# Fused attention and two mixtures of experts on one core: token norms from a Gram matrix, and a new order for the first tiles of the last layer

## Chip, cores and metric

The kernel runs on one core of one Trainium2 chip. The metric is the device time in microseconds (us) of one execution; lower is better. An execution's time is a little longer than the span from its first to its last instruction, which is what a trace shows.

## What is computed

Windowed attention (4 batches, 8 heads, 576 positions, 64 wide, window 64) gives x of 2304 tokens by 512. A first mixture of experts (8 experts with 4 slots each, 32 slots in all) turns x into slot outputs `so` and mixes them for each token. A second mixture sends each token to its best expert:

```python
# first mixture, its end
c = softmax(x @ phi, over the 32 slots)          # tokens x 32
y = c @ slot_out                                 # tokens x 512; slot_out is "so" below, 32 x 512
# second mixture
xn = y / (norm(y, per token) + 1e-6)
logits = xn @ en.T / tau                         # 8 experts
expert_idx = argmax(logits); gate_w = softmax(logits)[expert_idx]
for e in range(8):
    mask = expert_idx == e
    if not mask.any(): continue
    h = relu(y[mask] @ w1[e])                    # 512 -> 1024
    out[mask] = gate_w[mask, None] * (h @ w2[e]) # 1024 -> 512
```

All arithmetic is kept at about float32 accuracy: where a matmul runs on `fp32r` operands, one or both of them are split into a high and a low part.

## The kernel before

Work is ordered by hand (`tc.manual_schedule`): every engine runs its instructions in the order in which the code emits them. Attention comes first, with the first mixture's routing worked in; then its two layers, `layer1` (L709) and `layer2` (L729), in which the weights of all eight experts are streamed; then the second mixture. Only the stretch from `layer2` on is touched by the change.

**The combine matrix.** `c` (tokens by 32) lies in 18 tiles of 128 tokens. For each three tiles `prepT` (L792, VectorE) writes c divided by its sum, four times side by side, `trT` (L796) transposes it on TensorE, and `combT` (L802) writes it to `cTs` through `split_rows` (L701): a ScalarE copy of the high part, then one VectorE instruction which by row puts the high part or the remainder. `layer2(16)` to `layer2(31)` are 16 steps of four column-tiled matmuls each; the `combT` and `prepT` of tiles 6 to 11 stand between its steps 18 to 20 (L836 to L841), those of tiles 12 to 17 behind it. After `layer2`, `so` is copied out of PSUM (L845 to L847), and a short chain over TensorE and VectorE finds the expert `e0` of the first token. SyncE reads that number from SBUF (L895) and issues the loads of that expert's weights in five chunks `CH` (L877) of 1, 1, 2, 2 and 2 blocks of 128 hidden columns: `w1e` and `w2e` by turns (L897).

**The second mixture.** Since y = c @ so, the kernel doesn't form y for the layer. It takes u = so @ w1 instead (32 rows), and h = relu(c @ u). In `ffn` (L998) a chunk goes through these steps:
- `u_part` (L1002): four matmuls with 32 columns each, one for each quarter of the 512 inputs, that land in four groups of 32 rows; a copy to SBUF; `u_sum` (L1015) adds the groups with one more matmul by `R4` and splits the rows into `ust`. With chunk 0, `u_part` also forms so @ en (8 logit columns, L1010).
- `up` (L1022): for 256 tokens, one matmul of 256 columns for each hidden block, ReLU to the high part on ScalarE (or VectorE), and the low part on VectorE (L1032).
- `split_w2` (L1035): w2 into a high part (VectorE) and a low part (GpSimd).
- `down` (L1043): for one tile of 128 tokens and one chunk, three matmuls of 512 columns for each hidden block (high by high, low by high, high by low). `fin` (L1058) multiplies by the gate `gm` and stores.

**Norms and logits.** For each of the 18 tiles `ynorm` (L959) forms y with a matmul of 512 columns, and squares and sums it on ScalarE from PSUM, or from a copy in SBUF. `logits2` (L922) is a matmul of 8 columns a tile. `choose` (K), `others` (O), `gates` (G) and `gates_now` (M) are short chains on VectorE (with one small matmul and an Exp) that count which experts are used and make `gm`.

**The order.** The string `SEQ` (L9) names the steps for tiles 0 to 3 (and `up` for tiles 4 and 5): U, S, W and P, Q, R are `u_part`, `u_sum`, `split_w2` and `up` of token blocks 0, 1, 2, each taking its next chunk; 0 to 3 are `down` of that tile and chunk; a, b, d, y, z are norms and g logits. After the string tiles 4 to 17 follow, 24 matmuls each, in a fixed order that nothing in the change touches. PSUM has two buffers under each of the names `tr`, `s`, `et` and `pv`; tile 4 needs the `pv` buffer that `fin` of an earlier even tile frees.

Of the kernel before, what the change touches and what calls it, by code (L numbers as in the profile page):

```python
# [19 lines left out]
def tile_kernel(ctx, tc, q, k, v, phi, w1, w2, emb, tau, w1b, w2b, out):  # L20
# [21 lines left out]
    def ps(tag):  # L42
        return pp.tile([128, 512], FP32, tag=tag, name=tag)
# [55 lines left out]
    with tc.manual_schedule():  # L99
# [583 lines left out]
        sel = cpool.tile([128, 32], FP32, name="sel")  # L683
        selT = cpool.tile([32, 128], FP32, name="selT")

        sel5 = cpool.tile([128, 5, 32], F32R, name="sel5")
        selh = [sel5[:, i:i + 4] for i in range(2)]
# [10 lines left out]
        for r in range(5):  # L698
            g.tensor_scalar(out=sel5[:, r], in0=sel, scalar1=float(r % 2 == 0), scalar2=None, op0=ALU.mult)
# [68 lines left out]
        c4b = [md[:, 1124 + 384 * n:1508 + 384 * n].rearrange("p (t r s) -> p t r s", t=3, r=4) for n in range(2)]  # L768
# [23 lines left out]
        def prepT(t0):  # L792
            nc.vector.tensor_tensor(out=c4b[t0 // 3 % 2], in0=c[:, t0:t0 + 3, :].unsqueeze(2).to_broadcast([128, 3, 4, 32]),
                                    in1=cr[:, 1, t0:t0 + 3].unsqueeze(2).unsqueeze(3).to_broadcast([128, 3, 4, 32]), op=ALU.mult)

        def trT(t0):  # L796
            p = ps("et")
            for t in range(3):
                nc.tensor.transpose(p[:, 128 * t:128 * t + 128], c4b[t0 // 3 % 2][:, t].rearrange("p r s -> p (r s)"), ident)
            return p  # L800
# [26 lines left out]
        prepT(6)  # L827
        so_ps = ps("pv")
        layer2(16)
        combT(3, pT2)  # L830
        prepT(9)
# [27 lines left out]
        soT = m2.tile([128, 4, 2, 4, 4], FP32, name="soT")  # L859
        sos = wa.tile([128, 4, DM], F32R, tag=f"s{NA + 1}", name="sos")  # L860
        sost = sos[:, 0]
        soh = [sos[:, 1 + i] for i in range(2)]
# [21 lines left out]
        pT2 = trT(15) if "h" not in SEQ else None  # L884

        def rest9():
            combT(9)
            prepT(15)

# [30 lines left out]
        lg2 = []  # L920

        def logits2(t0, t1):  # L922
            if t0 == 0:
                lg2.append(ps("et"))
            l2p = lg2[0]
            for t in range(t0, t1):
                nc.tensor.matmul(l2p[:, E * t:E * t + E], lhsT=cTs[:, 128 * t:128 * t + 128], rhs=ust[0][:, 128:128 + E], start=True, stop=True)
            if t1 == NT:
                l2 = l2p[:, 0:E * NT].rearrange("p (t e) -> p t e", t=NT)
                nc.vector.tensor_reduce(out=mx, in_=l2, axis=AX.X, op=ALU.max)  # L930
                nc.vector.tensor_tensor(out=ld_, in0=l2, in1=mx.unsqueeze(2).to_broadcast([128, NT, E]), op=ALU.subtract)
# [27 lines left out]
        def ynorm(t, held=False, tag="tr"):  # L959
            p = ps("s" if held else tag)  # L960
            nc.tensor.matmul(p, lhsT=cTs[:, 128 * t:128 * t + 128], rhs=sost, start=True, stop=True)
            if held:
                nc.vector.tensor_copy(out=acc[:, t, :], in_=p)

                def square(dve):
                    if dve:
                        nc.vector.tensor_tensor_reduce(out=acc[:, t, :], in0=acc[:, t, :], in1=acc[:, t, :], scale=1.0, scalar=0.0,
                                                       op0=ALU.mult, op1=ALU.add, accum_out=nrm[:, t:t + 1])
                    else:
                        nc.scalar.activation(out=acc[:, t, :], in_=acc[:, t, :], func=ACTF.Square, accum_out=nrm[:, t:t + 1])  # L970

                return square
            nc.scalar.activation(out=p, in_=p, func=ACTF.Square, accum_out=nrm[:, t:t + 1])

# [12 lines left out]
        w2l = [wa.tile([128, 4, 512], F32R, tag=f"s{n}", name="w2l") for n in (4, 5)]  # L987
# [3 lines left out]
        ust = [m2.tile([128, 128 * n + (0 if f0 else E)], F32R, name=f"ust{f0}") for f0, n in CH]  # L991
# [6 lines left out]
        def ffn(first):  # L998
# [3 lines left out]
            def u_part(q_, dve=False):  # L1002
                f0, n = CH[q_]
                h, o = divmod(f0, 4)
                p = ps("tr")
                for cc in range(4):
                    l = soT[:, cc].rearrange("p r j i -> p (r j i)")
                    nc.tensor.matmul(p[32 * cc:32 * cc + 32, 0:128 * n], lhsT=l, rhs=w1e[h][:, cc, 128 * o:128 * (o + n)], start=True, stop=True)
                    if first and q_ == 0:
                        nc.tensor.matmul(p[32 * cc:32 * cc + 32, 128:128 + E], lhsT=l, rhs=enT[:, cc, :], start=True, stop=True)  # L1010
                w_ = 128 * n + (E if first and q_ == 0 else 0)
# [3 lines left out]
            def u_sum(q_, dve=False):  # L1015
                f0, n = CH[q_]
                p = ps("tr")
                w_ = 128 * n + (E if first and q_ == 0 else 0)
# [55 lines left out]
            yt = list(range(NT)) if first else []  # L1074
            yl = []

            lgs = [(t, t + 3) for t in range(0, NT, 3)]
            at = dict.fromkeys("USWPQRT/", 0)

            def ys(held, tag):  # L1080
                r_ = ynorm(yt.pop(0), held, tag)
                if r_:
                    yl.append(r_)

            def group(t):
                q_ = at["/"]
                down(t, range(CH[q_][0], sum(CH[q_])))
                if q_ == NQ - 1:
                    fin(t)

            def gates_now():
# [3 lines left out]
                "a": lambda: ys(False, "pv"), "b": lambda: ys(False, "tr"), "d": lambda: ys(True, "s"), "y": lambda: yl.pop(0)(False), "z": lambda: yl.pop(0)(True),  # L1095
                "g": lambda: logits2(*lgs.pop(0)), "h": rest9, "c": lambda: combT(12, pT), "C": lambda: combT(15, pT2),
                "K": choose, "O": others, "G": gates}
# [72 lines left out]
```

## Time and profile before

| | us |
|---|---|
| median of 3 runs | 299.7 |
| lowest and highest of them | 297.91, 301.16 |
| the profiled execution | 296.67 |
| its span | 295.0 |

Times in the rows count from the start of the span. A row of a timeline or a chain gives its start, its length, the engine, the line and what it did, with "x3" for three instructions merged; in brackets stands how long the engine had been idle and who released it. PE is TensorE's matmuls, PEld its weight loads (which overlap), DVE VectorE, ACT ScalarE, POOL GpSimd, SPq SyncE's queue. PEclk is the granted TensorE clock as a share of full speed. A float32 matmul shows as two instructions.

### The profile page before, as it was taken

Reading aid. Unit: us, or ns where it says so; the run is one execution under the profiler, and the core shown is the slowest. Engines: PE = TensorE matmul, PEld = TensorE weight load, DVE = VectorE, ACT = ScalarE, POOL = GpSimd, SP = SyncE. Lnnn points to the kernel's source line nnn. Section 1 sums busy time; section 2 is a strip of 40 time slices with the busy share of each in tenths; the row PEclk is TensorE's granted clock in tenths of the full one; section 3 lists DMA queues with packets and bytes.
Section 4 is the critical chain, followed back from the end, with each engine's and each line's share of the span. In section 5 each row is a group of like instructions: output and inputs, shape, how many; then the busy total and the mean of one; then the engine's idle time right before and its main releaser. Section 6 shows DMA issues by size and latency. Waiting matters only on the chain.

```text
span 295.0 us, 7567 instructions
## 1 busy us (share of the span) xinstructions
PE 274.2 (93%) x2860; PEld 209.1 (71%) x2860; DVE 173.7 (59%) x678; ACT 129.1 (44%) x351; POOL 61.8 (21%) x139
## 2 busy tenths in 40 slices
PE   7699899989998998999999799989999999999991
PEld 6477688878877886663432477768888888888891
DVE  4779787877897787554660488598333333333210
ACT  3775876687658776261210585440122112121100
POOL 4546524433405420040200033330000000000000
PEclk9999999999999999999999999999999999999998
DMA  5999899989999999999993394001231101010111
GB/s 134 280 231 296 255 274 306 306 247 278 278 341 308 280 299 378 366 376 390 387 386 131 95 337 143 0 0 50 95 67 41 38 36 71 36 38 36 72 48 32
DMA packets 53659, 57.26 MB, mean 194 GB/s; under 512 B 21490, under 2 KB 34034, under 8 KB 53618
## 3 DMA queue, kind: packets, MB, share of 16 engines
q1 hardware_dynamic: 53472, 56.70, 60.8%
q8 instruction: 25, 0.41, 0.6%
q14 instruction: 16, 0.13, 0.1%
q10 hardware_dynamic: 146, 0.02, 0.0%
HBM read 51.99 MB, written 4.72 MB: 192 GB/s over the span
## 4 chain that ended last, share of the span: by engine, by line
PE 70%; DVE 11%; ACT 9%; DMA 4%; SPq 2%; issue 2%; POOL 1%; POOLq 0%; ACTq 0%
PE et L1054 16%; PE pv L1054 15%; PE pv L732 5%; PE pv L325 5%; ACT sm L279 4%; PE tr L217 3%; PE s L1026 3%; PE tr L713 2%; PE s L713 2%; PE et L292 2%; ACT ets L298 2%; PE s L262 2%; PE pv L382 2%; DVE sm L278 2%; DMA v<-in_v_dram 2%
## 5 line engine op out<-in xcount | busy, mean ns | idle before, releaser
L279 ACT ACTIVATE sm<-sm,nm 128x128 f32<-128x128 f32 x144 | 47.3, 391 | 23.7 <-DVE nm L278 23.4
L1032 DVE SCALAR_TENSOR_TENSOR h<-s,h 128x512 fp32r<-128x512 f32 (+1 forms) x39 | 25.2, 650 | 43.4 <-ACT h L1031 43.1
L1031 ACT ACTIVATE h<-s 128x512 fp32r<-128x512 f32 (+1 forms) x33 | 18.8, 572 | 65.2 <-PE s L1026 65.0
L278 DVE CUSTOM_DVE_ANT_0 sm<-s,mask 128x128 f32<-128x128 f32 x144 | 34.1, 286 | 10.8 <-PE s L268 6.4
L1054 PE MATMUL pv<-w2h,h 128*128 128x512 f32 x144 | 37.4, 396 | 0.0
L1054 PE MATMUL et<-w2h,h 128*128 128x512 f32 (+1 forms) x160 | 37.1, 370 | 0.0
L1054 PEld LDWEIGHTS et<-w2h,h 128*128 128x128 f32 x160 | 27.4, 188 | 5.2 <-ACT h L1031 0.4
L325 PE MATMUL pv<-v,ets 128*64 128x65 f32 x640 | 25.7, 226 | 4.7 <-ACT ets L298 3.3
L1054 PEld LDWEIGHTS pv<-w2h,h 128*128 128x128 f32 x144 | 26.4, 188 | 5.0
L325 PEld LDWEIGHTS pv<-v,ets 128*64 128x64 f32 x640 | 21.4, 137 | 11.2 <-ACT ets L298 8.2
L217 PE MATMUL tr<-ident,spare 128*128 128x128 f32 x120 | 19.3, 285 | 2.1 <-POOL spare L212 2.1
L186 POOL COPY v<-v 64x512 f32<-64x512 f32 x16 | 9.7, 607 | 52.8 <-DMA v<-in_v_dram 52.8
L298 ACT COPY ets<-et 128x512 f32<-128x512 f32 x32 | 18.3, 572 | 3.5 <-PE et L292 3.1
L212 POOL COPY spare<-spare 128x512 f32<-128x512 f32 x30 | 18.3, 610 | 6.4 <-PE tr L217 4.1
L1054 PE MATMUL et<-w2l,h 128*128 128x512 f32 (+1 forms) x80 | 19.4, 368 | 0.0
L292 PE MATMUL et<-ident,sm 128*128 128x128 f32 x128 | 19.3, 273 | 0.0
L1054 PE MATMUL pv<-w2l,h 128*128 128x512 f32 x72 | 19.1, 390 | 0.0
L1039 POOL TENSOR_TENSOR w2l<-w2e,w2h 128x1024 fp32r<-128x1024 f32 (+1 forms) x5 | 9.8, 1952 | 37.5 <-PE tr L1019 20.7
L312 DVE COPY xT<-tr 128x320 f32<-128x320 f32 (+1 forms) x31 | 14.0, 451 | 4.3 <-ACT ets L300 3.6
L337 DVE TENSOR_TENSOR x<-pv,rc 128x256 f32<-128x256 f32 (+1 forms) x32 | 15.7, 491 | 1.1
L1026 PEld LDWEIGHTS s<-cTs,ust 128*128 128x128 f32 x72 | 13.0, 189 | 4.1 <-DVE h L1032 1.5
L1026 PE MATMUL s<-cTs,ust 128*128 128x256 f32 x72 | 14.7, 287 | 1.1 <-DVE h L1032 1.1
(313 smaller groups left out, 457.8 us busy)
## 6 DMA issues: line engine op xcount, KB each, us to landing
w<-in_moe_w_dram SPq DMA_DIRECT2D x32, 1024.0 KB, 8.5
v<-in_v_dram SPq DMA_DIRECT2D x32, 128.0 KB, 4.7
spare<-in_q_dram SPq DMA_DIRECT2D x15, 256.0 KB, 7.1
spare<-in_k_dram SPq DMA_DIRECT2D x15, 256.0 KB, 5.7
out_dram<-acc SPq DMA_DIRECT2D x15, 256.0 KB, 2.1
w1e<-in_moe_w_dram SPq DMA_DIRECT2D x3, 512.0 KB
w2e<-in_moe_w_dram SPq DMA_DIRECT2D x3, 512.0 KB, 7.6
out_dram<-acc SPq DMA_DIRECT2D x6, 128.0 KB, 2.1
```

Source lines behind the costliest of these rows:

```text
L212: g.tensor_copy(out=perm[nm], in_=t)
L217: nc.tensor.transpose(po[:, r], perm[nm][:, r].rearrange("p h d -> p (h d)"), ident)
L278: nc.vector.tensor_tensor_reduce(out=sm[:, u], in0=s[h][:, a], in1=m, scale=-scale, scalar=3.0e38, op0=ALU.add, op1=ALU.min, accum_out=nm[ ...
L279: nc.scalar.activation(out=sm[:, u], in_=sm[:, u], func=ACTF.Exp, bias=nm[:, u:u + 1], scale=-1.0)
L292: nc.tensor.transpose(p[:, 128 * u:128 * u + 128], e[:, u, :], ident)
L298: nc.scalar.copy(out=o[:, 0:4], in_=p.rearrange("p (n h q) -> p n h q", n=4, h=2))
L325: nc.tensor.matmul(p[64 * par:64 * par + 64, a, h, :], lhsT=et[:, u, x, :], rhs=vt[:, sl, h, :], start=True, stop=True)
L337: nc.vector.tensor_tensor(out=x_tok[b, hp][:, js[0]:js[0] + nj].rearrange("p j (h d) -> p j h d", h=2), in0=p[:, :, :, 0:64], in1=rc[:, 0: ...
L1026: nc.tensor.matmul(p[:, 256 * i:256 * i + 256], lhsT=ucol[f0 + i], rhs=cTs[:, 256 * NBS[nb]:256 * NBS[nb] + 256], start=True, stop=True)
L1031: nc.scalar.activation(out=av, in_=p, func=ACTF.Relu)
L1032: nc.vector.scalar_tensor_tensor(out=l[:, f0:f0 + n, :].rearrange("p f n -> p (f n)"), in0=p, scalar=0.0, in1=av.bitcast(FP32), op0=ALU.ma ...
L1054: nc.tensor.matmul(dps[t], lhsT=x[:, fc, o:o + 128], rhs=w[fc // 4][:, fc % 4, o_:o_ + w_], start=fc == 0 and i == 0, stop=fc == FC - 1 an ...
```

## The change

- `sel4` holds the slot selection four times, in float32. Four matmuls `so` by `sel4` give `esT`: `so` transposed, slots in all 128 rows' positions, with `en` beside it. Before, four transposes gave `soT`, and two matmuls of 512 columns gave `sost`.
- Four float32 matmuls of 40 columns give, for each slot, its 8 logits and its 32 products with all slots (the Gram matrix); `split_rows` writes them to `gst`.
- `logits2` is now a matmul of 40 columns a tile, six tiles at a time, with a ScalarE copy to SBUF. `norms` (L) makes from it, for half the tiles at a time on VectorE, the logits less their maximum, and the squared norm as sum over slots of (c G) times c. `ynorm` is gone, with all squares.
- For the chunks of one block (0 and 1), `u_part` is four accumulating float32 matmuls with all 128 columns of `esT`, and writes `ust` itself; only chunks 2 to 4 still have a `u_sum`.
- Tiles 6 to 17 of the combine matrix are transposed behind `layer2`, tiles 12 to 17 prepared first; two more buffers for `prepT` lie in a freed weight slot.
- `SEQ` is new: each tile counts its own chunks, and the steps of different tiles are mixed more finely. `f` is a matmul on the identity that nothing reads.

```diff
-SEQ = 'cdadWaUbdSadCuagPgagQagsWyuggqb0P21K3R/rbs0U1bWbpR3bSW2/Qy01QPbU3r2/bzsW2ORp01qy3/GM0123'
+SEQ = 'ggfUgffVQPU2WR1PW0U3RQ0S1U3LP2SQWUL1Q3S0WPK23P2Q10ORGM012R3R'
...
-        layer2(18)
-        for n in range(2):
-            if n < 1 or "h" not in SEQ:
-                combT(3 * n + 6)
-                prepT(3 * n + 12)
-            layer2(19 + n)
-        for t in range(21, 32):
+        prepT(6)
+        prepT(9)
+        for t in range(18, 32):
             layer2(t)
-        pT = trT(12)
+        pT = trT(6)
...
-        cp('v')(out=soh[0], in_=so)
-        nc.vector.tensor_tensor(out=soh[1], in0=so, in1=soh[0].bitcast(FP32), op=ALU.subtract)
-        ps_t = ps("s")
+        ps_t = [ps("s")[:, 0:256] for _ in range(2)]
         for cc in range(4):
-            nc.tensor.transpose(ps_t[:, 128 * cc:128 * cc + 128], so[:, 128 * cc:128 * cc + 128], ident)
-        p_so = ps("s")
-        for i in range(2):
-            nc.tensor.matmul(p_so, lhsT=selh[i].rearrange("p r s -> p (r s)"), rhs=soh[i], start=i == 0, stop=i == 1)
+            nc.tensor.matmul(ps_t[cc // 2][:, 128 * (cc % 2):128 * (cc % 2) + 128], lhsT=so[:, 128 * cc:128 * cc + 128], rhs=sel4.rearrange("p r s -> p (r s)"), start=True, stop=True)
+        combT(6, pT)
         for r in range(2):
-            cp('aa'[r])(out=soT[:, :, r], in_=ps_t.rearrange("p (c j r i) -> p c j r i", c=4, j=4, r=2)[:, :, :, r, 0:4])
-        cp('a')(out=sost, in_=p_so)
+            cp("av"[r])(out=esT[:, 2 * r:2 * r + 2, E:E + 128], in_=ps_t[r].rearrange("p (c s) -> p c s", c=2))
+        pT = trT(12)
+        combT(9, pT2)
+
+        p = ps("tr")[:, 0:E + 32]
+        for cc in range(4):
+            nc.tensor.matmul(p, lhsT=esT[:, cc, E:E + 128], rhs=esT[:, cc, 0:E + 32], start=cc == 0, stop=cc == 3)
+        split_rows(gst, p, neg_u)
+        pT2 = trT(15)
+        combT(12, pT)
+        combT(15, pT2)
...
         def logits2(t0, t1):
+            n = t1 - t0
+            p = ps("s" if t1 < NT else "et")[:, 0:(E + 32) * n].rearrange("p (t e) -> p t e", t=n)
+            for t in range(n):
+                nc.tensor.matmul(p[:, t], lhsT=cTs[:, 128 * (t0 + t):128 * (t0 + t) + 128], rhs=gst, start=True, stop=True)
+            nc.scalar.copy(out=lgs_[:, t0:t1], in_=p)
+
+        def norms(t0, t1):
+            n = t1 - t0
+            p = lgs_[:, t0:t1]
+            nc.vector.tensor_reduce(out=mx[:, t0:t1], in_=p[:, :, 0:E], axis=AX.X, op=ALU.max)
+            nc.vector.tensor_tensor(out=ld_[:, t0:t1], in0=p[:, :, 0:E], in1=mx[:, t0:t1].unsqueeze(2).to_broadcast([128, n, E]), op=ALU.subtract)
+            nc.vector.tensor_tensor(out=cg, in0=p[:, :, E:E + 32], in1=c[:, t0:t1], op=ALU.mult)
+            nc.vector.tensor_reduce(out=nrm[:, t0:t1], in_=cg, axis=AX.X, op=ALU.add)
             if t1 == NT:
+                nc.vector.tensor_tensor(out=nrm, in0=nrm, in1=cr[:, 1], op=ALU.mult)
+                nc.vector.tensor_scalar(out=nrm, in0=nrm, scalar1=0.0, scalar2=None, op0=ALU.max)
...
-        def ynorm(t, held=False, tag="tr"):
...
+                if n == 1:
+                    for cc in range(4):
+                        nc.tensor.matmul(p[:, 0:128], lhsT=esT[:, cc, E:E + 128], rhs=w1e[h][:, cc, 128 * o:128 * o + 128], start=cc == 0, stop=cc == 3)
+                    split_rows(ust[q_], p[:, 0:128], neg_u)
+                    return
```

## Rows read from the trace of the kernel before

**Rows 1.** Busy us, idle and clock by stage: length, engines' busy us (instructions), PEclk
```profile
163.00:169.00 6.00, 4.13 (x24) 2.21 (x22) 3.04 (x9) 3.42 (x10) 0.00 (x0) 1.00 0.27 82
169.00:206.10 37.10, 35.86 (x213) 28.15 (x213) 29.98 (x71) 17.43 (x50) 9.76 (x5) 1.00 0.31 107
206.10:289.00 82.90, 82.75 (x409) 70.01 (x407) 27.70 (x40) 14.37 (x24) 0.00 (x0) 1.00 0.16 54
...
292.00:293.00 1.00, 0.00 (x0) 0.00 (x0) 0.00 (x0) 0.00 (x0) 0.00 (x0) 0.67 0.04 10
```

**Rows 2.** Chain that ended last, around layer 2's end and the weights' arrival: start, us, what
```profile
151.95 0.48 PE et L799 x3
152.43 10.48 PE pv L732 x96
...
166.32 2.68 DMA w1e<-in_moe_w_dram
```

**Rows 3.** The same chain, prices of TensorE's steps and tile 4's start
```profile
172.75 0.23 PE et L927 x3
...
174.08 0.64 PE tr L1008 x8
...
176.75 0.70 PE pv L1054 x3
...
179.30 0.43 PE tr L1019 x2
...
184.90 0.24 PE s L1026 x2
185.13 1.36 PE pv L1054 x6
...
189.14 1.59 PE et L1054 x6
...
206.26 1.81 PE pv L1054 x8
```

**Rows 4.** Stages for the norms' matmuls (L961) alone: PE busy (instructions), PEld busy
```profile
163.00:169.00 6.00, 1.20 (x4) 0.67 (x4) 1.00 0.27 82
169.00:206.10 37.10, 5.42 (x14) 2.49 (x14) 1.00 0.31 107
```

**Rows 5.** Timeline of PE: float32 matmuls on the identity, and the stall
```profile
125.30 1.28 PE L113 MATMUL s<-ident 128*128 128x128 f32 x10
...
198.95 0.50 PE L1026 MATMUL s<-cTs,ust 128*128 128x256 f32 x2 [1.11 <-DVE h L1032]
```

**Rows 6.** Timelines of POOL and DVE: the last low part of w2, and VectorE beside it
```profile
194.66 2.40 POOL L1039 TENSOR_TENSOR w2l<-w2e,w2h 128x1024 fp32r<-128x1024 f32 x1 [6.27 <-DVE w2h L1038]
...
194.73 2.35 DVE L950 SCALAR_TENSOR_TENSOR used<-wgt,cur 128x8 f32<-128x8 f32 x1
197.12 0.17 DVE L951 TENSOR_TENSOR used<-used 128x8 f32<-128x8 f32 x1
```

**Rows 7.** Timelines of ACT and DVE: prices of their steps
```profile
163.46 0.61 ACT L847 COPY so<-pv 128x512 f32<-128x512 f32 x1
...
185.17 0.60 ACT L1031 ACTIVATE h<-s 128x512 fp32r<-128x512 f32 x1 [0.37 <-PE s L1026]
...
148.27 0.54 DVE L793 TENSOR_TENSOR s__2605<-s__2605 128x384 f32<-128x384 f32 x1
...
181.38 0.69 DVE L1038 CAST w2h<-w2e 128x1024 fp32r<-128x1024 f32 x1
...
191.72 0.69 DVE L1032 SCALAR_TENSOR_TENSOR h<-s,h 128x512 fp32r<-128x512 f32 x1
...
201.46 0.17 DVE L978 TENSOR_SCALAR nrm<-nrm 128x18 f32<-128x18 f32 x1
...
203.86 0.75 DVE L1063 TENSOR_SCALAR acc<-pv,gm 128x512 f32<-128x512 f32 x1
204.53 0.74 DVE L1063 TENSOR_SCALAR acc<-et,gm 128x512 f32<-128x512 f32 x1
```

More of the change, by code (lines that the diff above doesn't have):

```diff
@@ L682, in tile_kernel @@
         rot = cpool.tile([128, 4, 32], FP32, name="rot")
-        sel = cpool.tile([128, 32], FP32, name="sel")
+        sel4 = cpool.tile([128, 4, 32], FP32, name="sel4")
+        sel = sel4[:, 0]
         selT = cpool.tile([32, 128], FP32, name="selT")
-        sel5 = cpool.tile([128, 5, 32], F32R, name="sel5")
-        selh = [sel5[:, i:i + 4] for i in range(2)]
         for j in range(4):
@@ L697, in tile_kernel @@
             g.tensor_scalar(out=sel[rows, :], in0=ident[rows, 28 * j:28 * j + 32], scalar1=one_[rows, 0:1], scalar2=None, op0=ALU.mult)
-        for r in range(5):
-            g.tensor_scalar(out=sel5[:, r], in0=sel, scalar1=float(r % 2 == 0), scalar2=None, op0=ALU.mult)
+        g.tensor_copy(out=sel4[:, 1:4], in_=sel4[:, 0:1].to_broadcast([128, 3, 32]))
         def split_rows(dst, src, neg, eng=nc.scalar.copy):
@@ L826, in tile_kernel @@
         combT(0, pT)
-        prepT(6)
+        prepT(12)
         so_ps = ps("pv")
+        still = ps("pv")[:, 0:128]
         layer2(16)
         combT(3, pT2)
-        prepT(9)
+        prepT(15)
+        more = slot(NA + 1)([128, 2048])
+        c4b[2:4] = (more[:, 384 * n:384 * n + 384].rearrange("p (t r s) -> p t r s", t=3, r=4) for n in range(2))
+        cg = more[:, 768:768 + 16 * NT].rearrange("p (t s) -> p t s", t=NT // 2)
+        lgs_ = more[:, 768 + 16 * NT:768 + 16 * NT + (E + 32) * NT].rearrange("p (t e) -> p t e", t=NT)
         layer2(17)
@@ L858, in tile_kernel @@
         idx = m2.tile([128, 2], mybir.dt.int32, name="idx")
[L859 to L862, printed above, removed]
+        gst = m2.tile([128, E + 32], F32R, name="gst")
+        esT = m2.tile([128, 4, E + 128], FP32, name="esT")
+        g.tensor_copy(out=esT[:, :, 0:E], in_=enT)
         mx = m2.tile([128, NT], FP32, name="mx")
@@ L883, in tile_kernel @@
         nc.vector.tensor_copy(out=k0b, in_=p[:, 0:4])
[L884 to L888, printed above, removed]
+        pT2 = trT(9)
         l0 = ps("tr")[0:1, 0:E]
@@ L1005, in u_part @@
                 p = ps("tr")
-                for cc in range(4):
[L1007 to L1011, printed above, removed]
+                if n == 1:
[3 more added lines that the diff above has]
+                    return
+                for cc in range(4):
+                    nc.tensor.matmul(p[32 * cc:32 * cc + 32, 0:128 * n], lhsT=esT[:, cc, E:E + 32], rhs=w1e[h][:, cc, 128 * o:128 * (o + n)], start=True, stop=True)
+                w_ = 128 * n
                 us[q_] = m2.tile([128, 256], FP32, tag="us", name="us", bufs=2)
@@ L1017, in u_sum @@
                 p = ps("tr")
-                w_ = 128 * n + (E if first and q_ == 0 else 0)
+                w_ = 128 * n
                 nc.tensor.matmul(p[:, 0:w_], lhsT=R4, rhs=us.pop(q_)[:, 0:w_], start=True, stop=True)
@@ L1072, in fin @@
                         nc.sync.dma_start(out=out[r0:r0 + 64, :], in_=acc[64 * i:64 * i + 64, t, :])
[L1074 to L1083, printed above, removed]
+            lgs = [(0, NT // 3), (NT // 3, 2 * NT // 3), (2 * NT // 3, NT)]
+            nms = [(0, NT // 2), (NT // 2, NT)]
+            at = dict.fromkeys("UWPQR0123", 0)
+            at["S"] = sum(n == 1 for _, n in CH)
             def group(t):
-                q_ = at["/"]
+                q_ = at[str(t)]
+                at[str(t)] += 1
                 down(t, range(CH[q_][0], sum(CH[q_])))
@@ L1094, in ffn @@
             once = {
[L1095 to L1097 removed]
+                "g": lambda: logits2(*lgs.pop(0)), "f": lambda: fill(still, 1), "L": lambda: norms(*nms.pop(0)), "K": choose, "O": others, "G": gates}
             step = {
[L1099 to L1102 removed]
+                "U": u_part, "S": u_sum, "W": split_w2, "V": lambda n: split_w2(n, nc.vector.tensor_copy, nc.vector),
+                "P": lambda n: up(0, *CH[n]), "Q": lambda n: up(1, *CH[n]), "R": lambda n: up(2, *CH[n])}
             for x in SEQ:
@@ L1106, in ffn @@
                 elif x in step:
[L1107 removed]
+                    X = "W" if x == "V" else x
                     step[x](at[X])
```

36 lines of the change are left out of this document (5 added, 31 removed).

## The prediction

> **What bounds the kernel now.** I read the stages first, then the chain of work that ended last, then each engine's timeline between 147 and 207 us. From 206.10 to the end of the matmuls TensorE is busy 82.75 of 82.90 us, and in the 37.10 us before that 35.86 [rows 1]: TensorE's own instruction stream sets the end. The last 14 tiles (4 to 17) are untouched, so whatever the change is worth is read at one point, the start of tile 4 at 206.1 [rows 3]. Everything later moves with it, and the end of the span too. Ahead of that stand three pieces where TensorE isn't the limit: layer 2 ends at 152.43 + 10.48 = 162.91, the first expert's first weights arrive at 166.32 + 2.68 = 169.00 [rows 2], between them TensorE is busy 4.13 of 6.00 us [rows 1]; and at 197.8 it stands still for 1.11 us behind VectorE [rows 5], which had an 8-column instruction take 2.35 us where its neighbour takes 0.17 [rows 6].
>
> **Layer 2's end.** Two transposes of three tiles stand inside layer 2, on TensorE's chain, 0.48 us each (one of the two rows stands) [rows 2]. They leave it, so layer 2 ends 0.96 us earlier, at 161.95. The VectorE work that went with them (`prepT`, 0.54 us each [rows 7]) runs beside 10 us of layer 2 and costs nothing. The expert's number, SyncE's read and its ten loads all move with layer 2's end; nothing new stands ahead of them on SyncE's queue. So the first weights land near 169.00 - 0.96 = 168.05.
>
> **From layer 2's end to the first u_part.** What TensorE must do before it, in order, now includes the Gram path. The copy of `so` ends at 163.46 + 0.61 - 0.96 = 163.1 [rows 7]; the expert's matmuls are out at 163.45. Then four float32 matmuls of 128 columns. Their price: ten single instructions took 1.28 us, 0.13 each with the last one's run-out in it, and a float32 matmul is two, so 1.0 at most for four that follow closely [rows 5]; from above 1.7, four times the 0.43 that a lone one of 256 columns holds the chain [rows 3]. I take 0.95, by the row of the same shape, less a little for the run-out. So 164.4. Two copies to `esT` (about 0.4 each, ScalarE and VectorE side by side, behind `combT(6)`) end at 164.95. The transpose of tiles 12 to 14 fits in that wait. Four matmuls of 40 columns: 8 instructions of 0.13, to 166.0; two steps of split, to 166.55; the last transposes lie inside that. Then twelve tiles of logits and one `f`. Three tiles of 8 columns hold the chain 0.23 us [rows 3], 0.077 a tile; that is weight loading, and 40 columns should fit under it. From above I bound it by 0.12 a tile, an `up` matmul of 256 columns (0.24 for two) [rows 3]. With run-out and `f` that is 1.4 to 1.7 us: u_part(0) can start at 168.25. The weights (168.05) and the work (168.25) arrive together; before, it started at 169.04. Gain 0.8.
>
> **From u_part(0) to tile 4 on TensorE.** Four tiles of `down`: each 2 x 0.70 + 3 x 1.36 = 5.48, so 21.9. 24 `up` matmuls of 0.12: 2.8. u_part(0) and (1): 2 x 0.95 = 1.9. u_part(2) to (4): 3 x 0.6 = 1.8 (row of 0.64). u_sum(2) to (4): 3 x 0.45 = 1.35. Six tiles of logits 0.75, two `f` 0.5, the matmul of O 0.25. Sum 31.3 [rows 3]. After a column-tiled u_part the next `down` takes about 0.2 longer (1.59 instead of 1.36 [rows 3]); three times, 0.6. So TensorE could begin tile 4 at 168.25 + 31.3 + 0.6 = 200.2. The same prices summed over the old order give 34.3 plus the stall of 1.1, against 37.06 measured from 169.04: they leave 1.6 unexplained, in small waits. I keep that for the range.
>
> Where the difference comes from: 14 of the 18 norm matmuls lay in that stretch [rows 4], 0.23 each, 3.2 us; twelve logits tiles go into the wait for weights, 0.9 to 1.4; two u_sums go, but the longer u_part of a one-block chunk takes that back and 0.5 more; `f` costs 0.5.
>
> **VectorE at the end of the string.** ScalarE loses all squares, and its new copies of 240 columns (under 0.6 [rows 7]) are hidden beside `down`. VectorE is the engine to follow. Its instructions read the norms' parts from SBUF now. By columns between 0.17 (8) and 0.54 (384) [rows 6, 7], one half of `norms` is 0.23 + 0.23 + 0.45 + 0.43 = 1.35, the second half 0.35 more. The first half, at 177.6, lies between two `down` groups. The second comes right behind the `split_w2` of chunk 3 (cast 0.69 [rows 7], at 182.1 to 182.8), so beside a GpSimd instruction of 2.40 us. In the trace the two-input instruction that started 0.07 us after such a GpSimd instruction ended when that one ended, 194.73 + 2.35 = 197.08 against 194.66 + 2.40 = 197.06; the next took 0.17 [rows 6]. I take it that the subtraction of `norms` waits like that, to 185.3, and ends at 186.75; the low part of Q's chunk 3 (0.69 [rows 7]) at 187.4, where tile 3 wants it at 187.7. Then the sum of chunk 4, the cast of chunk 4 (188.55), P's chunk 3, and `choose`, which waits again for GpSimd to 191.05 and ends at 192.75; two more low parts to 194.1; O's chain, 1.6 without its stall, to 195.7; R's chunk 2 to 196.4; G and M, 201.46 to 203.86 before [rows 7], 2.4, to 198.8. Three `fin` at 0.67 apart (203.86, 204.53 [rows 7]) free `pv` for tile 4 at 200.8. TensorE is ready at 200.2, so it waits 0.6 to 0.7 and tile 4 starts near 200.9. The old stall of 1.1 is gone, a smaller one has come.
>
> A rule bears on this. The Trainium skill, "SBUF — State Buffer", section "Who interferes with whom", says that a VectorE instruction with two SBUF inputs and a GpSimd instruction that reads SBUF exclude each other, and the later one waits to the end of the first; the 2.35 us row agrees. By that rule `norms` and `choose` wait, as the sum has it; without it VectorE would be ahead by some 2 us at 187, but O's place in TensorE's order would hold the gates to within 0.3 us of the same time. It speaks against the change at one place, Q's chunk 3, which is the second rival.
>
> **The sum.** Tile 4 moves from 206.1 to 200.9: 5.2 us. The profiled execution would go from a span of 295.0 to 289.8. The runs' median, 299.7, is 3.0 above the profiled execution's 296.67; taking the same 5.2 off it gives 294.5.
>
> **The rivals.**
> 1. *TensorE alone sets it.* O and G come early enough, and logits cost nothing beyond their weight loads: the wait of 0.7 and the 0.6 vanish. Gain 6.5, 293.2. For it: 35.86 of 37.10 busy [rows 1]. Against it: three `fin` in a row follow M whatever comes before.
> 2. *VectorE becomes the bound.* Q's chunk 3 is ready 0.3 us before it is wanted. If `norms` takes 0.5 longer a half or GpSimd holds VectorE a little longer, every matmul behind it slides. It decides from 0.3 us on; 1.5 us of slide leaves 3.7, 296.0. For it: VectorE is busy 29.98 of 37.10 already [rows 1].
> 3. *The norms were filler.* Without matmuls that depend on nothing, TensorE waits at the short early steps (ust to `up` to ReLU to low part to `down`, four hops between 169 and 176). If all 3.2 us of the removed norms turn into waits, the gain is 2.0, 297.7: the change then does not do what it says. Against it: my walk finds each operand 0.2 to 1.4 us before its use.
> 4. *Slower, by the clock.* The granted clock is 1.00 in every stage up to 289, and fell to a mean of 0.67 in 292 to 293, when no matmul had run since 289 [rows 1]. If the thinner work between 162 and 169 let it fall to 1.2 GHz, each us of work would take two. It beats the gain when more than 5.2 us of work run so; 8.5 us would end at 303. Against it: TensorE had 1.87 us idle there before, at full clock [rows 1], and now has less.
>
> **How the numbers follow.** Chances: forecast (gain 4.4 to 6.2) 0.48, rival 1 0.12, rival 2 (2.5 to 4.4) 0.22, rival 3 (up to 2.5) 0.13, rival 4 0.05. Faster by over 1% (about what a measurement of this kernel can tell from none) means a gain over 3.0: the forecast, rival 1 and three quarters of rival 2, 0.76. Within 1%: the rest of rival 2 and rival 3, 0.19. Slower: 0.05. The predicted time is 294.5. The range goes from rival 1 less the small costs that I bounded from above (292.6) to rival 3's 297.9; it leaves out the clock and part of rivals 1 and 3. The forecast's own range is 293.5 to 295.3.
>
> **What would show it.** Right: layer 2's last matmul at 162.0; the first u_part at 168.0 to 168.5 with no long wait for weights; no matmul of 512 columns between them; granted clock 1.00; tile 4 at 200 to 201.5, its first matmul released by `fin` on VectorE. A two-input VectorE instruction of `norms` or `choose` that takes over 2 us beside a GpSimd row shows the wait. Wrong: tile 3's chunk 3 waiting for VectorE (rival 2), many short waits of `down` for `up` before 177 (rival 3), or a clock below 1.00 before 289 (rival 4).

## The result, and the profile after

The changed kernel takes 291.58 us (median of six executions, 290.68 to 293.1) beside 299.78 us for the kernel before (297.91 to 303.05): a ratio of 0.973, 95% interval 0.969 to 0.977, 8.2 us. Two later comparisons of the same pair give 292.02 (ratio 0.980, 0.976 to 0.984) and 291.83 (0.974, 0.968 to 0.980). The sign and the place of the gain are as forecast; the time is 0.6 to 1.0 us below the low end of the range and 2.9 us below the forecast of 294.5. The profiled execution went from 296.67 to 290.68 us, its span from 295.0 to 289.0.

The chain of work of the changed kernel from layer 2 to tile 4 (start, length, what):

```profile
148.26 1.85 PE pv L729 x16
...
150.42 12.20 PE pv L729 x112
...
164.10 1.10 PE s L903 x8
...
165.75 0.83 PE tr L912 x8
...
167.23 1.49 PE s L923 x12
168.72 0.31 PE pv L113 x2
169.03 0.89 PE tr L999 x8
...
171.28 0.94 PE tr L999 x8
...
200.46 0.24 PE s L1019 x2
200.70 1.82 PE pv L1047 x8
```

In the chain of before, layer 2 starts with this row:

```profile
147.32 1.85 PE pv L732 x16
```

Layer 2 starts 0.94 us later than there, although nothing ahead of it is changed. So the comparison is made from there: layer 2's start to the first matmul of tile 4 was 206.26 - 147.32 = 58.94 us [rows 3], and is 200.70 - 148.26 = 52.44 us. That is 6.50 us. Less the 0.94 by which layer 2 starts later, and with 0.4 gained behind the start of tile 4 (a part that takes 88.3 to 88.7 us in either kernel), it makes the 6.0 of the span.

The stages that answer to [rows 1] (stretch, length, busy us of PE, PEld, DVE, ACT and POOL with instructions, granted clock, DMA share, GB/s):

```profile
162.60:169.00 6.40, 5.96 (x52) 5.07 (x53) 3.42 (x10) 3.93 (x11) 0.00 (x0) 1.00 0.31 76
169.00:200.70 31.70, 31.70 (x180) 25.63 (x179) 25.31 (x61) 11.74 (x27) 8.48 (x4) 1.00 0.37 119
200.70:283.00 82.30, 82.30 (x409) 69.92 (x407) 29.04 (x42) 14.96 (x25) 0.00 (x0) 1.00 0.16 56
```

Between layer 2 and the first `u_part` TensorE now idles 0.44 us, where it idled 1.87 [rows 1]; from there to the end of the matmuls it is busy without a gap. VectorE lost 4.7 us in the second stage, ScalarE 5.7. The GpSimd timeline has these three rows (start, length, engine, line, operation, tiles; in brackets the idle time before and what ended it):

```profile
176.47 2.39 POOL L1032 TENSOR_TENSOR w2l<-w2e,w2h 128x1024 fp32r<-128x1024 f32 x1 [1.86 <-DVE w2h L1031]
183.24 2.40 POOL L1032 TENSOR_TENSOR w2l<-w2e,w2h 128x1024 fp32r<-128x1024 f32 x1 [4.38 <-DVE mx L930]
188.67 2.40 POOL L1032 TENSOR_TENSOR w2l<-w2e,w2h 128x1024 fp32r<-128x1024 f32 x1 [3.03 <-DVE w2h L1031]
```

The VectorE timeline beside these rows and around the first three `fin`, with the same columns:

```profile
176.57 0.76 DVE L1025 SCALAR_TENSOR_TENSOR h<-s,h 128x256 fp32r<-128x256 f32 x2 [0.18 <-ACT h L1024]
178.45 0.50 DVE L931 TENSOR_TENSOR ld<-s__2716,mx 128x72 f32<-128x72 f32 x1
...
183.03 0.22 DVE L930 TENSOR_REDUCE mx<-s__2716 128x9 f32<-128x72 f32 x1
183.28 2.45 DVE L931 TENSOR_TENSOR ld<-s__2716,mx 128x72 f32<-128x72 f32 x1
...
189.11 2.13 DVE L941 SCALAR_TENSOR_TENSOR oh<-ld,wgt 128x144 f32<-128x144 f32 x1
...
198.63 0.24 DVE L1080 SCALAR_TENSOR_TENSOR gm<-kmax,cur,gate 128x18 f32<-128x18 f32 x1
198.97 0.75 DVE L1056 TENSOR_SCALAR acc<-pv,gm 128x512 f32<-128x512 f32 x1
199.63 0.74 DVE L1056 TENSOR_SCALAR acc<-et,gm 128x512 f32<-128x512 f32 x1
200.29 0.75 DVE L1056 TENSOR_SCALAR acc<-pv,gm 128x512 f32<-128x512 f32 x1
```

And TensorE's timeline at the same point:

```profile
200.30 0.40 PE L1019 MATMUL s<-cTs,ust 128*128 128x256 f32 x2
200.54 1.98 PE L1047 MATMUL pv<-w2h,h 128*128 128x512 f32 x8
```

Tile 4 begins at 200.54 (200.70 on the chain) in `pv`, while the third `fin`, which reads `pv` too, runs until 201.04. It needed the first one only, over at 199.72.

### The profile page after: what moved, and what is told of

The parts are those of the page before. It is cut to its first block, busy times and chain, and to the rows that moved or that the text cites. A ratio compares the mean times of both kernels' runs of the same rounds, so it can differ in the third digit from the quotient of the medians.

```text
span 289.0 us, 7506 instructions
## 1 busy us (share of the span) xinstructions
PE 270.9 (94%) x2846; PEld 209.0 (72%) x2846; DVE 169.4 (59%) x670; ACT 123.7 (43%) x328; POOL 60.4 (21%) x135
## 4 chain that ended last, share of the span: by engine, by line
PE 73%; ACT 9%; DVE 7%; DMA 3%; SPq 2%; issue 2%; POOL 1%; POOLq 0%; ACTq 0%
PE et L1047 17%; PE pv L1047 17%; PE pv L325 5%; PE pv L729 5%; ACT sm L279 4%; PE tr L217 4%; PE s L1019 3%; PE tr L710 3%; PE s L710 2%; PE et L292 2%; ACT ets L298 2%; PE pv L382 2%; PE s L262 2%; DMA v<-in_v_dram 2%; DVE sm L278 2%
## 5 line engine op out<-in xcount | busy, mean ns | idle before, releaser
L1024 ACT ACTIVATE h<-s 128x512 fp32r<-128x512 f32 (+1 forms) x39 | 21.8, 565 | 68.7 <-PE s L1019 68.7
L1047 PE MATMUL pv<-w2h,h 128*128 128x512 f32 x144 | 36.8, 392 | 0.0
L217 PEld LDWEIGHTS tr<-ident,spare 128*128 128x128 f32 x120 | 12.6, 140 | 4.1 <-POOL spare L212 2.2
L1047 PEld LDWEIGHTS et<-w2l,h 128*128 128x128 f32 x80 | 13.7, 189 | 2.1
```

The lines of the kernel that those rows point to most:

```text
L217: nc.tensor.transpose(po[:, r], perm[nm][:, r].rearrange("p h d -> p (h d)"), ident)
L1024: nc.scalar.activation(out=av, in_=p, func=ACTF.Relu)
L1047: nc.tensor.matmul(dps[t], lhsT=x[:, fc, o:o + 128], rhs=w[fc // 4][:, fc % 4, o_:o_ + w_], start=fc == 0 and i == 0, stop=fc == FC - 1 an ...
```

## The experiments

The stretch from layer 2's start to tile 4, by the chain, is what each run is read by; "clock" is TensorE's granted clock, 1.00 for 2.4 GHz and 0.50 for 1.2. A number of runs stands for the timed executions of that kernel; ratios are to the kernel before, run beside it.

**Is one profiled execution of before typical?** The kernel before, unchanged, four more times.

> The kernel before, unchanged, to get another profiled execution and more timed ones. In its first profiled execution layer 2 began at 147.3 us and tile 4 at 206.3, a stretch of 58.9 us; the changed kernel's took 52.4 us (148.3 to 200.7). Theory A (the change is worth the 6.5 us of that stretch, and the rest of the 8 us between the medians is that the profiled execution before was a quick one in its part ahead of layer 2): the stretch is 58.9 within 0.3 again, and what differs lies ahead of 147 us. Theory B (most executions of the kernel before lose one or two us more inside the stretch, in the wait for the first weights or by the clock): the stretch is 60 or more, with the loss between 163 and 170 us or a granted clock below 1.00.

> The kernel before, a further profiled execution. Two so far: the stretch from layer 2's start to tile 4 was 58.9 us at full clock and 59.6 with half clock from 168 to 171.5. Clock theory: in most further ones the granted clock falls behind the wait for the weights, with a stretch of 59.5 to 61. Rival (what the median holds beyond the first profiled execution lies ahead of layer 2): the stretch is 58.9 to 59.2 at full clock and layer 2 starts at 148 to 150 instead of 147.3.

> The kernel before, one more profiled execution, for the same question. Clock theory: half clock behind the wait for weights, stretch 59.5 to 61 us. Rival: full clock there, stretch 58.9 to 59.2, layer 2 later than 147.3.

> The kernel before, a last profiled execution, for the same question. Clock theory: half clock behind the wait for weights, stretch 59.5 to 61 us. Rival: full clock there, stretch 58.9 to 59.2, layer 2 later than 147.3.

The stretch took 59.57, 60.85, 59.74 and 59.72 us, against the 58.94 of the execution on which the prediction was built: that one was the quickest of five. It was the quickest ahead of the stretch too: layer 2 began at 147.32 us there, and at 147.96, 149.18, 150.50 and 147.94 in the others. (Timed again, the unchanged kernel gave a ratio of 0.999, 0.996 to 1.002.) No expectation came as it was put: the clock fell in two of the four, not in most, and the two at full clock were longer than 59.2. The excess has two faces. In the first two the clock fell where TensorE's work is thin, between layer 2's end and the expert's weights, at 168.0 and 168.8. Stages of the second of them:

```profile
166.00:168.00 2.00, 1.52 (x12) 0.88 (x10) 1.41 (x5) 0.33 (x2) 0.00 (x0) 1.00 0.05 12
168.00:169.00 1.00, 0.36 (x1) 0.04 (x1) 0.00 (x0) 0.60 (x2) 0.00 (x0) 0.91 0.02 8
169.00:175.00 6.00, 5.96 (x35) 3.87 (x36) 4.07 (x7) 4.03 (x12) 1.27 (x1) 0.50 0.92 295
175.00:178.00 3.00, 3.00 (x23) 2.70 (x27) 1.53 (x4) 2.24 (x7) 0.00 (x0) 0.89 1.03 369
```

TensorE was busy 0.36 of the 1.00 us before 169, and then 5.96 of 6.00 us at 1.2 GHz. In the other two the clock was 1.00 from layer 2 on, but the second `u_part` has a wait that the first profile did not have, 0.66 and 0.63 us. TensorE's timeline of the last of the four (in brackets the idle time before, and what ended it):

```profile
172.22 0.43 PE L1008 MATMUL tr<-w1e,soT 128*32 128x128 f32 x8 [0.63 <-ACT pv L973]
```

The bracket names a norm's square on ScalarE (L973), but that isn't what it waited for. In the first profile the same `u_part` began while the same square had just begun:

```profile
170.80 0.58 ACT L973 ACTIVATE pv<-pv 128x512 f32<-128x512 f32 x1
...
170.86 0.43 PE L1008 MATMUL tr<-w1e,soT 128*32 128x128 f32 x8
```

It waited for the second chunk of weights. By the trace's semaphore records that load landed 2.99 us after its issue in the first profile, and 3.59 and 3.85 us after it in these two, 0.1 us ahead of the `u_part`. In the last of the four the third chunk was late as well, and the chain goes through its load (`169.35 6.04 DMA w1e<-in_moe_w_dram`). The 1.11 us stall of [rows 5] is in all five.

**Does the changed kernel repeat?** Unchanged, three more times.

> The changed kernel, unchanged. Theory A: ratio to the kernel before 0.973 to 0.980, the stretch from layer 2's start to tile 4 is 52.4 within 0.3, and what varies lies ahead of layer 2. Theory B: the stretch is as steady as that too, since its first u_part no longer waits for weights, but the kernel before varies there. The ratio alone does not tell them apart, the traces do.

> The changed kernel, a further profiled execution. Clock theory: full clock from 162 on, the stretch 52.4 within 0.2. Rival: as it varies ahead of layer 2, layer 2 starts anywhere from 147.3 to 150, with the same stretch. Both can hold together; the kernel before tells them apart.

> The changed kernel unchanged, beside after_fill_gram on the same chip. 291 to 293 us, ratio 0.972 to 0.981; one or two executions of the set with a clock under 0.985 and 2 to 4 us longer, as in after_third. A set without any such execution would speak for a clock that depends on the chip.

Stretches of 52.43, 56.23 and 52.77 us; layer 2 began at 147.72, 150.23 and 148.11. The 56.23 lost the clock, against its expectation: this stage answers to the one above.

```profile
172.00:178.00 6.00, 6.00 (x29) 5.90 (x29) 2.15 (x6) 1.55 (x5) 0.00 (x0) 0.50 0.96 314
```

So the changed kernel is not free of it, and lost more in this one execution: 3.8 us, 0.34 of it a wait within layer 2, where before lost 1.1 (60.85 against 59.7) with the clock at 0.50 for about as long. A likely reason, not tested, is that it has no waits left in which half speed would be hidden. Among the six timed executions of the last of these runs, the two with a mean clock under 0.985 took 297.3 and 293.54 us, the other four 290.1 to 292.91.

In the 52.77 the second `u_part` came out of a wait for its weights. Chain:

```profile
167.32 3.85 DMA w1e<-in_moe_w_dram
...
171.21 1.16 PE tr L999 x8
```

That costs some 0.3 us here, less than in before, since the loads go out earlier. SyncE's issue of the same load, before (first row) and after:

```profile
167.55 0.37 SPq L900 DMA_DIRECT2D w1e<-in_moe_w_dram  x1
...
167.34 0.37 SPq L893 DMA_DIRECT2D w1e<-in_moe_w_dram  x1
```

From layer 2's start that is 20.23 us before and 19.08 after. In the first profile of the changed kernel the load landed 3.67 us after its issue, as late as in the slower ones of before, and TensorE did not idle.

**Are the norms' matmuls worth 3.2 us by themselves?** All steps of the norms leave the old order; `nrm` is set to 1.

```diff
-SEQ = 'cdadWaUbdSadCuagPgagQagsWyuggqb0P21K3R/rbs0U1bWbpR3bSW2/Qy01QPbU3r2/bzsW2ORp01qy3/GM0123'
+SEQ = 'cWUSCugPggQgsWuggq0P21K3R/rs0U1WpR3SW2/Q01QPU3r2/sW2ORp01q3/GM0123'
...
+        g.memset(nrm, 1.0)
```

> The kernel before without its 18 norm matmuls and their squares: the steps a, b, d, y and z are taken out of the order and nothing is put in their place; the norms are set to 1, so the gates are not those of the reference. Theory of the prediction (14 matmuls of 0.23 us lay on TensorE's stream): 3.2 us less, 296.5 us, ratio 0.989. Rival (they were filler for waits): less than 1 us, ratio over 0.996. Rival (ScalarE and VectorE were held up by the squares too, so more comes back): 5 us or more, ratio under 0.983.

301.74 us, ratio 1.010 (1.006 to 1.013): less work and slower, which none of the three expectations had, with a stretch of 63.1 us. Stages:

```profile
166.00:170.00 4.00, 1.01 (x18) 0.71 (x17) 0.80 (x2) 0.97 (x2) 0.00 (x0) 0.97 0.53 175
170.00:182.00 12.00, 10.09 (x54) 7.90 (x49) 5.34 (x15) 2.08 (x6) 2.53 (x2) 0.50 0.87 292
```

TensorE idled 3 of 4 us ahead of the weights, and the next 12 us ran at 1.2 GHz. To separate the clock from the waits, the next run adds matmuls on the identity that nothing reads, eight behind the matmuls by `sel` and six, as `f`, around the first two `u_part`s:

```diff
-SEQ = 'cWUSCugPggQgsWuggq0P21K3R/rs0U1WpR3SW2/Q01QPU3r2/sW2ORp01q3/GM0123'
+SEQ = 'cWffUSffCffugPggQgsWuggq0P21K3R/rs0U1WpR3SW2/Q01QPU3r2/sW2ORp01q3/GM0123'
...
+        fill(still, 8)
```

> The kernel before without its norm matmuls and squares, as before_no_norms (gates not those of the reference), with matmuls on the identity in the waits: eight ahead of the first weights, four by the first u_parts. before_no_norms was 2 us slower than the kernel before, with a clock of 0.50 from 170 to 182. Clock theory: the clock holds, and the removal then shows its own price, 3 us less than the kernel before, ratio 0.985 to 0.992. Rival (the waits for weights and for the short early steps take what the norms leave, at any clock): ratio 0.997 to 1.005.

300.49 us, ratio 1.000 (0.995 to 1.005), stretch 60.40. The clock now holds until 178, and the time goes to a wait for the third chunk's weights instead. Chain, and a stage behind it:

```profile
170.24 6.50 DMA w1e<-in_moe_w_dram
...
176.88 0.64 PE tr L1011 x8
```

```profile
178.00:180.00 2.00, 2.00 (x8) 1.71 (x8) 1.37 (x4) 0.00 (x0) 0.00 (x0) 0.51 1.07 375
```

The old order without norms runs ahead into weights that have not landed, and TensorE idles 1.71 us ahead of them. The wait and the clock are not told apart in full: behind the wait the clock falls again, from 178.1 to 181.5. Half of these 3.4 us, 1.7, is an estimate of what that costs. Without it the stretch would be 58.7 us, 0.2 to 1.0 less than the full-clock executions of before (58.94 to 59.74). So by this estimate at most 1.0 of the 3.2 us of matmuls taken out came back.

**Does filling alone help before?** Three fills and two `f`, nothing removed.

```diff
-SEQ = 'cdadWaUbdSadCuagPg
+SEQ = 'cdadWaffUbdSadCuagPg
...
+        fill(still, 3)
```

> The kernel before with five matmuls on the identity that nothing reads (0.24 us each): three behind the last matmul by sel, where TensorE waits for a copy, and two ahead of the first u_part, where it waits for weights. In its second profiled execution the granted clock was 0.50 from 168 to 171.8 us, right behind that wait; in the first it stayed at 1.00. Clock theory (the runs' median of the kernel before holds such a fall in part, and the changed kernel's busy wait avoids it): granted clock 1.00 from 163 to 175, 0.7 to 2 us faster than the kernel before, ratio 0.993 to 0.998. Rival (the clock is not what the median holds beyond the profiled execution): same time or up to 0.5 us slower, ratio 0.999 to 1.002.

300.35 us, ratio 1.000 (0.995 to 1.005); the profiled stretch 59.31 at full clock. Neither expectation can be told from the other at this width: inconclusive.

**Order or parts?** The changed kernel with its steps in the old order.

```diff
-SEQ = 'ggfUgffVQPU2WR1PW0U3RQ0S1U3LP2SQWUL1Q3S0WPK23P2Q10ORGM012R3R'
+SEQ = 'ggfWUgffUPQWUQ0P21LLK3RRS0U1WPR3SW2Q01QPU3R2SW2ORP01Q3GM0123'
```

> The changed kernel with the steps of its string in the old order (norm letters and the sums of chunks 0 and 1 left out, the first split of w2 back on VectorE and GpSimd ahead of the first u_part, both halves of L where the last logits were, the three f kept). Theory A (the order carries a large part of the 6.5 us, since the old order without norms waits for the second and third chunk of weights: a wait of 1.5 and one of 1 us in before_no_norms): 2 to 4 us slower than the changed kernel, with TensorE waiting between 169 and 178 us and again at O. Theory B (the parts of the steps carry it, the order little): under 1 us slower.

298.35 us, ratio 0.997 (0.993 to 1.001); stretch 57.38, all at full clock. So in the old order the new parts gain 1.56 of the 6.50 us, and the new order brings the other 4.94, more than either theory had. Three waits make 3.8 of it. Chain, and the stages around the first two:

```profile
169.07 5.16 DMA w1e<-in_moe_w_dram
...
174.27 0.64 PE tr L1003 x8
...
194.56 2.25 DVE used L956
...
198.67 0.50 PE s L1019 x2
```

```profile
172.00:174.30 2.30, 1.16 (x14) 0.96 (x14) 1.07 (x4) 0.83 (x3) 0.87 (x1) 1.00 1.00 320
180.00:185.00 5.00, 3.40 (x20) 2.59 (x17) 4.24 (x14) 1.83 (x4) 1.81 (x1) 1.00 0.14 51
```

The third chunk's weights (1.14 us of idle in 172 to 174.3), then VectorE with `norms` and `choose` in a row (TensorE 3.40 of 5.00 busy, VectorE 4.24), then the old stall of 1.08 us at O, with an 8-column instruction of 2.25 us as in [rows 6]. The other 1.1 stands in no wait of these.

**Does TensorE's stream alone set the end now?** Fourteen independent matmuls of 512 columns (as the norms' were) put back among the steps of the new order, as `n`.

```diff
-SEQ = 'ggfUgffVQPU2WR1PW0U3RQ0S1U3LP2SQWUL1Q3S0WPK23P2Q10ORGM012R3R'
+SEQ = 'ggfUgffVQPU2nWnR1nPnW0nU3nRnQ0nS1nU3nLP2nSQWUL1nQ3nS0nWPK23nP2nQ10nORGM012R3R'
...
+            def idle_norm():
+                nc.tensor.matmul(ps("tr"), lhsT=cTs[:, 0:128], rhs=w2h[0][:, 0, :], start=True, stop=True)
```

> The changed kernel with 14 matmuls of 512 columns put back among its steps (as many as the norms had in the old stretch; nothing reads what they write, and no other engine does anything for them). The norms' matmuls came out of the kernel before at no gain (before_no_norms_filled: ratio 1.000), where three steps waited for weights. Theory A (in the new order TensorE's stream alone sets the end from the first u_part on, so each matmul counts): 3.0 to 3.6 us slower than the changed kernel, 14 x 0.23 with small change. Theory B (the new order too has waits that such matmuls fill): under 1.5 us slower.

295.73 us, ratio 0.989 (0.983 to 0.996); stretch 55.87, 3.43 more, 14 times 0.245 us, where one holds the chain for 0.23 to 0.24. Chain of it:

```profile
171.58 0.70 PE pv L1047 x3
172.28 0.23 PE tr L1083
```

In the new order, a us of TensorE is a us of the end. In the old order 3.2 us of it were worth 1.0 at most, by the estimate above. And the order alone isn't the gain either: with these matmuls in it, the new order is 3.07 us shorter than before (58.94 - 55.87), not 6.50.

**Does it matter that the transposes left layer 2?** Two of them go back between layer 2's first tiles, in the changed kernel; a second run fills the thinner place behind layer 2 (three fills and two more `f`, which the lines below do not show).

```diff
-        for t in range(18, 32):
+        layer2(18)
+        for n in range(2):
+            combT(3 * n + 6)
+            layer2(19 + n)
+        for t in range(21, 32):
...
```

> The changed kernel with the transposes and splits of tiles 6 to 11 back between steps 18 to 20 of layer 2, and those of tiles 12 to 17 right behind it. Theory of the prediction: layer 2 ends 0.96 us later, the first weights arrive 0.96 us later, the work ahead of the first u_part shrinks by as much and then waits for the weights; 0.2 to 1.0 us slower than the changed kernel. Rival (the wait for weights has a margin of 1 us or more, so the place of the transposes is free): within 0.2 us of the changed kernel.

> after_comb_in_layer2 with five more matmuls on the identity: three while the split of the Gram matrix is waited for, two ahead of the first u_part. It was 4.2 us slower than the changed kernel, of which its profile shows some 3.3 us at half clock (173.4 to 180 us) and 1.3 us of a later first u_part. Clock theory: the clock holds, and it is 1.0 to 1.6 us slower than the changed kernel. Rival (the place of the transposes itself costs 4 us): still 3.5 us or more slower.

Unfilled 296.2 us (ratio 0.990, 0.986 to 0.994), stretch 57.04, much more than the 0.2 to 1.0 expected; filled 293.56 us (0.979, 0.973 to 0.986), stretch 53.91. Unfilled, the clock falls behind the thin place:

```profile
170.00:171.00 1.00, 0.48 (x5) 0.52 (x5) 0.26 (x1) 0.08 (x1) 0.00 (x0) 1.00 0.13 36
...
173.00:180.00 7.00, 7.00 (x32) 6.61 (x31) 2.81 (x7) 1.90 (x6) 0.78 (x1) 0.51 0.97 303
```

Filled, it stayed at 1.00. So of the 4.6 us 1.5 are left with the clock held (the place of the transposes and the fills' own time), and 3.1 came back with it; by the medians of the runs it is 1.5 and 2.6, from 292.0, the changed kernel beside the unfilled run. (The profiled unfilled execution was the slowest of its six.)

**And in before?** The same two transposes and their `prepT` moved behind layer 2, in the kernel before.

```diff
-            if n < 1 or "h" not in SEQ:
-                combT(3 * n + 6)
-                prepT(3 * n + 12)
...
+        combT(6, pT)
+        prepT(12)
+        combT(9, pT2)
+        prepT(15)
```

> The kernel before with one part of the change alone: the transposes and splits of tiles 6 to 11 leave layer 2 and stand behind it, between the copy of sost and the first norms. Step of the prediction: layer 2 ends 0.96 us earlier and the first weights land 0.96 earlier; the stretch from layer 2's start to tile 4 is 58.0 instead of 58.9, 0.5 to 1 us faster (ratio 0.9965 to 0.999). Rival (the wait just grows elsewhere, or the splits on ScalarE and VectorE hold up the norms): no gain, ratio 0.9995 or more. A fuller wait also keeps the clock: then more than 1 us, ratio under 0.996.

299.93 us, ratio 1.004 (1.001 to 1.008); stretch 60.3: no gain. The first load did go out 1.26 us earlier, 17.74 us after layer 2's start instead of 19.00. But behind layer 2 the norms' operands came late, behind a `prepT` that the change itself does earlier, and the clock fell. So the run doesn't price that step of the prediction by itself:

```profile
166.00:168.00 2.00, 0.01 (x1) 0.04 (x1) 1.24 (x3) 1.11 (x3) 0.00 (x0) 1.00 0.59 175
168.00:173.00 5.00, 5.00 (x36) 3.70 (x40) 4.29 (x9) 3.61 (x11) 0.00 (x0) 0.66 0.84 262
```

**What are the `f` for, and would more help?** First the changed kernel without its three `f`, then with one fill more, behind the transpose of tiles 15 to 17.

```diff
-SEQ = 'ggfUgffVQPU2WR1PW0U3RQ0S1U3LP2SQWUL1Q3S0WPK23P2Q10ORGM012R3R'
+SEQ = 'ggUgVQPU2WR1PW0U3RQ0S1U3LP2SQWUL1Q3S0WPK23P2Q10ORGM012R3R'
```

```diff
         pT2 = trT(15)
+        fill(still, 1)
```

> The changed kernel without its three f steps. As plain work they hold TensorE for 0.31 + 0.54 = 0.85 us in its profile. Plain theory: 0.5 to 0.9 us faster than the changed kernel. Clock theory: the clock falls to 0.50 behind the wait in most executions, 1 to 4 us slower.

> The changed kernel with one more matmul on the identity (0.24 us), in the 0.31 us in which TensorE waits for the split of the Gram matrix. Clock theory: it costs nothing and the granted clock falls behind the wait in fewer executions, so 0 to 1 us faster than after_fourth beside it and a mean clock of at least the same. Rival (one matmul there changes nothing that decides the clock): within 0.4 us, same clocks.

Without `f` 293.9 us (ratio 0.981, 0.975 to 0.988): some 2 us above the changed kernel's median, though the intervals of the ratios overlap. The profiled stretch is 53.63, 1.2 us longer with 0.85 us less on TensorE's chain (0.31 and 0.54), and its stages say why:

```profile
170.00:172.00 2.00, 1.84 (x13) 1.74 (x12) 1.37 (x3) 1.01 (x4) 0.00 (x0) 0.71 0.94 245
172.00:174.00 2.00, 2.00 (x10) 1.90 (x9) 0.93 (x4) 0.54 (x3) 0.00 (x0) 0.50 1.03 350
```

With one fill more the stretch is 52.55 and the time 292.33 us (0.975, 0.970 to 0.980), beside 291.83 for the changed kernel: no difference that can be measured. No version better than the changed kernel was found.

## Why the prediction was right and where it was wrong

**Right: the mechanism.** All but 0.4 us of the profiled gain lies between layer 2 and tile 4, as forecast, and later work only moved with it. The first `u_part` came 20.77 us after layer 2's start (169.03 - 148.26), forecast 20.93. TensorE's sum from there to tile 4, 31.9 by prices from the old trace, measured 31.67. Layer 2 took 14.36 us, forecast 14.63. The Gram path's terms hold singly within 0.4: 1.10 for the four float32 matmuls against 0.95, 0.83 against 1.05 for the next eight, 1.80 for twelve logits tiles and `f` against 1.4 to 1.7. In the last one 40 columns did not fit under the price of 8: 1.49 us for twelve is 0.124 a tile, against 0.077.

**Right: the waits for GpSimd.** The subtraction in the second `norms` took 2.45 us and ended at 185.73, 0.09 behind a GpSimd instruction of 2.40 us from 183.24; the first instruction of `choose` that reads two SBUF tiles took 2.13 (0.30 in the run with the old order, with GpSimd idle) and ended at 191.24, 0.17 behind the next one, from 188.67. The first `norms` shows a short one that the prediction didn't have: its subtraction took 0.50 (0.23 in that run) and ended at 178.95, 0.09 behind the GpSimd instruction from 176.47. Two low parts that began within that same GpSimd instruction, at 176.57, with one input in PSUM, took 0.76 together, no longer than two at 171.62 without GpSimd (0.76). The Trainium skill, "SBUF — State Buffer", section "Who interferes with whom", makes exactly that difference (two SBUF inputs, not one), and the four rows agree. The waits cost nothing: Q's chunk 3 was not held, so rival 2 did not come.

**Wrong, first step: "Three `fin` [...] free `pv` for tile 4 at 200.8".** Against layer 2's start, tile 4 came 1.14 us earlier than the sum said (52.44 against 200.9 - 147.32 = 53.58). TensorE was 0.4 earlier than its own sum; the other 0.7 is the wait for VectorE, which did not occur. Two terms were off in it: the chain to `gm` ended 0.87 earlier, measured from layer 2, than forecast (198.87 against 198.8 + 0.94), and tile 4 took the buffer that the first `fin` had freed. Which `fin` frees which buffer could have been counted from the rotation of `pv` and `et`. Fourteen matmuls put back and paid for in full show that TensorE's stream alone sets the end, which is rival 1. That its 6.5 is met to the first decimal is luck: of the 0.6 that it let go with the wait only 0.4 came, and the prediction counted from 206.1 where the chain has 206.26.

**Wrong, second step: "taking the same 5.2 off" the median.** Of the 2.9 us between forecast and result 0.8 lies in the profiled gain (5.2 forecast, 6.0 measured: the first step's 1.1, less layer 2's later start, and smaller parts), 2.1 in this step. It held that after would stand to its own profiled execution as before did, 3.0 us above. It stands 0.9 above. The profiled execution of before was the quickest of five, ahead of layer 2 (by 0.6 to 3.2 us) and in the stretch. At full clock two others took 59.7 us there, and against the three full-clock executions of after (52.43 to 52.77) that is a gain of 7.0 to 7.3, not 6.5. In those two the second chunk's weights landed 0.6 and 0.9 us later after their issue than in the first; after has such landings too (3.67 and 3.85 in two of its four executions), but issues its loads 1.15 us earlier, counted from layer 2's start. That reading rests on these few traces and no run tests it alone. The medians of the three comparisons lie 8.2, 7.3 and 7.5 us apart; what is left over the 7.0 to 7.3 is within the interval of the first (6.9 to 9.4) and isn't settled.

**Wrong in part, the attribution.** "14 of the 18 norm matmuls [...] 3.2 us" was booked as gain by itself. In the old order their removal gave back 1.0 at most: they filled waits, as rival 3 said, but of the old order. In the new order it is worth its price (3.43 when matmuls like them are put back). So removal and order make the gain together: the parts without the order gain 1.56, the order with the matmuls 3.07, both 6.50. The sum priced TensorE's stream rightly, and did not name the order as what makes the stream count.

**Rival 4, the clock.** It was priced for the changed kernel alone. Five executions of before fell to half speed there in two, four of after in one: too few to say which loses it more often, and no run shows what decides it within a kernel. What the runs show is that small work at this place can hold it: three fills and two `f` gave back 2.6 us, and without the three `f` the profiled stretch was 2.0 us longer than its work accounts for.

A slip in the range changes nothing: its upper end is called rival 3's 297.9, where that rival says 297.7.

## What to carry to other kernels

Before booking removed work as gain, ask what in its stage the removed work covers: without it, waits for weights may appear, and half the clock behind them. Only in an order in which every operand comes early does a removed us count. Profile the kernel before several times and build the sum on a typical execution: the quickest one hides waits that most others have.

## What the runs showed of the hardware

The clock of TensorE differs between executions of one program at the same place: between layer 2's end and the second `u_part` it stayed at 1.00 or fell to 0.50, in both kernels. It does so in the first 15 us too, which the change doesn't touch: 0.89 there in four of the five executions of before and two of the four of after, 1.00 in the others. So the mean clock of an execution (median 0.988 over 90 of before, 0.993 over 19 of after) doesn't tell at which place it was lost, and how much of the 8.2 us is the clock's stays open.

The time from a weight load's issue to its landing differs as well. The first chunk's ended 2.68 us after its issue [rows 2], the second's 2.99 to 3.85 in the executions of the two kernels. The third's, a load of twice the size, ended 5.16 to 6.50 us after its issue where the chain waits for it. The ten loads are issued one behind the other, about 0.6 us apart at first.
